# K and Q in rows of 4 or 2 tokens, reordered on the way out of PSUM; the first two FFN blocks interleaved; sink values over the SP queue

## The chip, the cores and the metric

The kernel runs on one core of a Trainium2 chip. The metric is the device time in microseconds. One execution is also taken by the hardware profiler; its span runs from the first to the last thing that the profile shows. The engines are PE (matmul; PEld is its weight load), DVE (vector), ACT (scalar), POOL and SP; each runs its own instructions in order and waits at semaphores for the others.

## The reference

Windowed attention with sinks, then a gated FFN. In short:

```python
# q, k, v: (4, 8, 768, 64); n_sink = 4, window = 128
scores = matmul(q, k^T) / sqrt(64)
keep   = (pos_k < n_sink) | ((0 <= pos_q - pos_k) & (pos_q - pos_k < window))
a      = softmax(where(keep, scores, -1e9));  attn = matmul(a, v)
x      = attn.transpose(0, 2, 1, 3).reshape(3072, 512)
g      = x @ w_gate                      # (512, 1536)
out    = (g * sigmoid(g) * (x @ w_val)) @ w_out   # (3072, 512), float32
```

Inputs are float32; the loads on POOL's queue cast them to bf16.

## The kernel before

**Attention.** The 3072 tokens are 12 groups of 256 (`NG`), three for each of 4 batches; group g has batch `b` and place `c`. For a group, `load_group` (L89, L96) loads K, Q and V with one token on each partition, so that one row read from memory is 64 floats, 256 bytes. Then come, per pair of heads p where nothing else is said:

- `step_T` (L206): four 128x128 transposes of K and Q into one PSUM tile `pt`, evicted by ACT (L213) or, for odd p before the FFN begins, by DVE (L211) into `kqT`, which holds features on partitions and the 768 tokens of a batch in order.
- `step_ks` (L221, L223), once a batch: sink columns of K into `ks`, and `vsb` = `vc` times `diag_h`, a block-diagonal copy of the sink rows of V. `vc` is loaded by 32 small loads (L185) behind all others that are issued before the FFN.
- `step_S` (L242): scores in one two-bank PSUM tile `s`, exponential on ACT (L247), mask on DVE (L251).
- `step_K` (L261, L266): scores of the sinks for a group with c > 0, and their exponential `es`.
- `step_PV` (L286), four a group: the weighted sum of V, with sums of weights from a column of ones in `va`; reciprocal and scaling on DVE (L291, L292) into `xn`.
- `step_X` (L304), two a group: transposes `xn` back to `xT` (L307), the FFN's input.

**FFN.** A block has 512 tokens, two groups. It has 12 `gate` units (four matmuls `pg` L340, tanh on ACT L343, four matmuls `pv` L348, then `u` L352 and `ht` L353 on DVE) and 4 `down` units (12 matmuls `pd` L363, eviction on ACT L367, store on SP L368). `pg`, `pv` and `pd` share three PSUM tiles, `ps_f`. Gate weights come in four chunks of three units, `wo` in four.

**Order.** All is written out by hand: `tc.manual_schedule()` leaves the engines' orders as the code issues them. Groups 0 and 1 run first, alone. Then, while block tb runs, the steps of groups 2tb+2 and 2tb+3 stand in its 16 units, by a list `slots`; within a gate they stand between pg and pv. DVE work of a step goes to `later` and is issued at the unit's end (`flush`), but evictions L211 and L213 are issued in place. The loads are issued on POOL in this order: group 0, group 1, gate weights, group 2, `wo`, group 3, `vc`; groups 4 and up when the transposes of the group four before are done. Eight loads of POOL's queue can be under way.

Of the kernel before, what the change touches and what calls it, by code (L numbers as in the profile page):

```python
# [15 lines left out]
def kernel(  # L16
# [26 lines left out]
    TB = 512  # L43
    NTB = NTOK // TB
    VS = 72
    FG = 3
# [10 lines left out]
    natp = pool("natp", 4)  # L57
    vpool = pool("vpool", 1)
    kqtp = pool("kqtp", 2)
    epool = pool("epool", 3)  # L60
# [3 lines left out]
    xtp = pool("xtp", 2)  # L64
# [6 lines left out]
    ps_o = pool("ps_o", 2, True)  # L71
    ps_t = pool("ps_t", 1, True)
# [6 lines left out]
    def load_group(g, split=1):  # L79
        b, c = divmod(g, GC)  # L80
        t0 = c * 256
        kq = natp.tile([P, 2, 2, H * D], BF16, tag="kq", name="kq")
        va = vpool.tile([P, 2, H, VS], BF16, tag=f"va{g}", name="va")
        hn = H // split
        for s in range(split):
            hs = slice(s * hn, (s + 1) * hn)
            for i, src in ((0, k), (1, q)):
                for j in range(2):
                    nc.gpsimd.dma_start(  # L89
                        kq[:, i, j, s * hn * D:(s + 1) * hn * D].rearrange(  # L90
                            "p (h d) -> p h d", d=D),
                        src[b, hs, t0 + j * P:t0 + (j + 1) * P].rearrange(
                            "h p d -> p h d"),
                    )
        for j in range(2):
            nc.gpsimd.dma_start(  # L96
                va[:, j, :, 0:D],
                v[b, :, t0 + j * P:t0 + (j + 1) * P].rearrange("h p d -> p h d"),
            )
        nat[g], vas[g] = kq, va  # L100
# [3 lines left out]
    def load_gate(i):  # L104
        n = FG * P
        for lst, w, nm in ((wgs, moe_w_gate, "wg"), (wvs, moe_w_val, "wv")):
            t = wpool.tile([P, DMC, n], BF16, tag=f"{nm}{i}", name=nm)
            nc.gpsimd.dma_start(
                t, w[:, i * n:(i + 1) * n].rearrange("(c p) f -> p c f", p=P))
            lst.append(t)  # L110
# [14 lines left out]
    vcs, vsbs, kss = [], [], []  # L125

    load_group(0, split=2)
    make_identity(nc, ident)


    def build_mask(m, sink):
# [19 lines left out]
    load_group(1)  # L151
    build_mask(mask0, True)
    load_gate(0)
    load_gate(1)
    build_mask(mask, False)
    load_gate(2)
    load_gate(3)
    load_group(2)


    nc.gpsimd.memset(diag_h, 1.0)
    nc.gpsimd.affine_select(
        out=diag_h, in_=diag_h, compare_op=ALU.is_ge, fill=0.0, base=0,
        pattern=[[-NS, H]], channel_multiplier=1)
    nc.gpsimd.affine_select(
        out=diag_h, in_=diag_h, compare_op=ALU.is_ge, fill=0.0, base=NS - 1,
        pattern=[[NS, H]], channel_multiplier=-1)
    KS = P + 2 * NS
    for b in range(B):
        vc = const.tile([P, D + 1], BF16, tag=f"vc{b}", name="vc")  # L170
        nc.vector.memset(vc, 0.0)
        nc.vector.memset(vc[:, D:D + 1], 1.0)
        ks = const.tile([P, NP2 * KS], BF16, tag=f"ks{b}", name="ks")
        nc.vector.memset(ks, 0.0)
        vsb = const.tile([P, H, D + 1], BF16, tag=f"vsb{b}", name="vsb")
        vcs.append(vc)
        kss.append(ks)
        vsbs.append(vsb)

    for i in range(4):  # L180
        load_out(i)
    load_group(3)
    for b in range(B):
        for h in range(H):
            nc.gpsimd.dma_start(vcs[b][h * NS:(h + 1) * NS, 0:D], v[b, h, 0:NS])  # L185

    def ones_v(g):
        nc.vector.memset(vas[g][:, :, :, D:D + 1], 1.0)
# [10 lines left out]
    def step_T(g, p, on_dve=False):  # L199
        b, c = divmod(g, GC)  # L200
        if c == 0 and p == 0:
            kqT[b] = kqtp.tile([P, NP2, 2, S], BF16, tag="kqT", name="kqT")
        pt = ps_t.tile([P, 2, 2, P], BF16, tag="pt", name="pt")
        for i in range(2):
            for t in range(2):
                nc.tensor.transpose(  # L206
                    pt[:, i, t], nat[g][:, i, t, p * P:(p + 1) * P], ident)
        dst = kqT[b][:, p, :, c * 256:(c + 1) * 256].rearrange(
            "q i (t r) -> q i t r", t=2)
        if on_dve:  # L210
            nc.vector.tensor_copy(out=dst, in_=pt)  # L211
        else:
            nc.scalar.copy(out=dst, in_=pt)  # L213

    def step_ks(g):

        b = g // GC
        dst = kss[b].rearrange("q (a m) -> q a m", m=KS)
        for h in range(2):
            r = slice(h * D, (h + 1) * D)  # L220
            nc.vector.tensor_copy(  # L221
                out=dst[r, :, h * NS:(h + 1) * NS], in_=kqT[b][r, :, 0, 0:NS])
        nc.vector.tensor_tensor(  # L223
            vsbs[b],
            vcs[b].rearrange("q (o d) -> q o d", o=1).broadcast_to([P, H, D + 1]),
            diag_h.rearrange("q (h o) -> q h o", o=1).broadcast_to([P, H, D + 1]),
            op=ALU.mult)
# [27 lines left out]
    def step_K(g):  # L255
# [3 lines left out]
        ps = ps_t.tile([P, 256], FP32, tag="pt", name="pk")  # L259
# [8 lines left out]
    def step_PV(g, j, hh):  # L268
# [4 lines left out]
        po = ps_o.tile([P, 4, D + 1], FP32, tag="o", name="o")  # L273
# [23 lines left out]

    def step_X(g, j):
        tb, off = divmod(g * 256 + j * P, TB)
        if off == 0:  # L300
            xTs[tb] = xtp.tile([P, DMC, TB], BF16, tag="xT", name="xT")
        pt = ps_t.tile([P, DMC, P], BF16, tag="pt", name="px")
        for i in range(DMC):
            nc.tensor.transpose(pt[:, i], xns[g, j][:, i * P:(i + 1) * P], ident)  # L304

        def dve():
            nc.vector.tensor_copy(out=xTs[tb][:, :, off:off + P], in_=pt)  # L307
        later.append(dve)

    def T(g, p):  # L310
        def f(pro=False):
            if p == 0:
                ones_v(g)
            step_T(g, p, on_dve=(pro and p % 2 == 1))
            if p == NP2 - 1:
                if g % GC == 0:
                    later.append(lambda: step_ks(g))
                if g + 4 < NG:
                    load_group(g + 4)
        return f  # L320

    def A(fn, *a):
        def f(pro=False):
            if pro and fn is not step_S:
                flush()
            fn(*a)
        return f
# [4 lines left out]
    def gate(tb, f, attn):  # L332
        fi, fo = divmod(f, FG)
        fs = slice(fo * P, (fo + 1) * P)
        if f == 0:
            hts[tb] = hpool.tile([P, DFC, TB], BF16, tag="ht", name="ht")
        x = xTs[tb]
        pg = ps_f.tile([P, TB], FP32, tag="f", name="pg")
        for c in range(DMC):
            nc.tensor.matmul(pg, wgs[fi][:, c, fs], x[:, c],  # L340
                             start=(c == 0), stop=(c == DMC - 1))
        th = tpool.tile([P, TB], FP32, tag="th", name="th")
# [3 lines left out]
        pv = ps_f.tile([P, TB], FP32, tag="f", name="pv")  # L346
        for c in range(DMC):
            nc.tensor.matmul(pv, wvs[fi][:, c, fs], x[:, c],  # L348
                             start=(c == 0), stop=(c == DMC - 1))

        u = upool.tile([P, TB], BF16, tag="u", name="u")
        nc.vector.scalar_tensor_tensor(u, th, 1.0, pg, op0=ALU.add, op1=ALU.mult)  # L352
        nc.vector.tensor_tensor(hts[tb][:, f], u, pv, op=ALU.mult)  # L353
        flush()

    def down(tb, ts, attn):
        po = ps_f.tile([P, DM], FP32, tag="f", name="pd")
        n = DFC // 4
        for f in range(DFC):
            if f == DFC // 2:  # L360
                for a in attn:
                    a()
# [5 lines left out]
        nc.sync.dma_start(out[tb * TB + ts * P:tb * TB + (ts + 1) * P], ot)  # L368
        flush()


    def run(*steps):
        for s in steps:
            s(pro=True)
# [3 lines left out]
    def ts(g):  # L378
        return [T(g, p) for p in range(NP2)], [A(step_S, g, p) for p in range(NP2)]

    def px(g):
        return ([A(step_PV, g, j, hh) for j in range(2) for hh in range(2)],
                [A(step_X, g, j) for j in range(2)])

    t0, s0 = ts(0)
    t1, s1 = ts(1)
    v0, x0 = px(0)
    v1, x1 = px(1)
    run(*t0)
    run(s0[0], s0[1], s0[2], t1[0], s0[3], t1[1], t1[2], t1[3])  # L390
    run(v0[0], s1[0], v0[1], s1[1], v0[2], s1[2], v0[3], s1[3],
        A(step_K, 1), x0[0], x0[1])
    run(*v1, *x1)
    flush()
    for tb in range(NTB):
        slots = [[] for _ in range(16)]
        if tb + 1 < NTB:
            ga, gb = 2 * tb + 2, 2 * tb + 3
            ta, sa = ts(ga)
            tb_, sb = ts(gb)  # L400
            va_, xa = px(ga)
            vb, xb = px(gb)
            slots = [
                [ta[0], ta[1]], [ta[2], ta[3]], [sa[0]], [sa[1], A(step_K, ga)],
                [sa[2], tb_[0]], [sa[3], tb_[1]], [va_[0], tb_[2]],
                [va_[1], tb_[3]], [va_[2], sb[0], A(step_K, gb)], [va_[3], sb[1]],
                [xa[0], sb[2]], [xa[1], sb[3]],
                [vb[0], vb[1]], [vb[2], vb[3], xb[0]], [xb[1]], [],
            ]
        for f in range(DFC):  # L410
            gate(tb, f, slots[f])
        for s in range(TB // P):
            down(tb, s, slots[DFC + s])
# [35 lines left out]
```

The softmax here doesn't subtract the row's maximum and nothing guards it: scores larger than these inputs give would overflow.

## Time and profile before

| | |
|---|---|
| runs (us) | 329.96, 330.28, 327.13; median 329.96 |
| profiled execution | 327.02 us, span 325.2 us |
| granted TensorE clock | 1.00 |
| busy of the span: PE, PEld, DVE, ACT, POOL | 77%, 40%, 52%, 39%, 29% |
| chain that ended last | PE 63%, DVE 13%, DMA 9%, POOL 7%, ACT 5%, issue 2% |
| DMA | 85268 packets, of which 76544 under 512 bytes; HBM read 28.34 MB, written 6.29 MB |

Shares of busy time are means over the span; the page's second part has the span in 40 slices and shows where the work lies. In a row of groups the two last numbers before the second bar are busy time in all and the mean of one instruction. In the chain a row is start, length and what ran.

### The profile page before, as it was taken

How to read it: one execution, taken by the hardware profiler on the slowest of the kernel's cores; microseconds unless marked ns; L12 is line 12 of the kernel's file. 1: busy time of each engine (PE TensorE's matmuls, PEld its weight loads, DVE VectorE, ACT ScalarE, POOL GpSimd, SP SyncE). 2: the span in 40 equal slices, each digit the busy share in tenths (PEclk: the TensorE clock that was granted, in tenths of full speed). 3: DMA queues.
4: the chain of work that ended last, by engine and by line, in shares of the span. 5: the costliest groups of instructions: out<-in, count | busy, mean ns of one | idle time of the engine just before them, and what ended most of it. 6: DMA issues, size and time to landing. Idle time of an engine off the chain costs nothing.

```text
span 325.2 us, 4622 instructions
## 1 busy us (share of the span) xinstructions
PE 251.2 (77%) x1824; PEld 128.8 (40%) x1824; DVE 167.9 (52%) x352; ACT 127.2 (39%) x197; POOL 95.8 (29%) x142
## 2 busy tenths in 40 slices
PE   0420000576999988999979999799997999999995
PEld 0210000353454544555434545345453454544442
DVE  2200000663788526886158882378842688617830
ACT  1230000324665136762257541475514666223321
POOL 8996756996532006050042600000000000000000
PEclk9999999999999999999999999999999999999999
DMA  8999999099929129390149932100011000020002
GB/s 56 113 132 203 173 203 90 1 72 124 100 15 84 40 92 73 24 99 30 69 54 78 75 24 90 39 2 3 1 65 67 0 2 0 34 94 3 2 32 97
DMA packets 85268, 20.75 MB, mean 64 GB/s; under 512 B 76544, under 2 KB 82176, under 8 KB 85248
## 3 DMA queue, kind: packets, MB, share of 16 engines
q0 software_dynamic: 81792, 14.18, 55.3%
q1 hardware_dynamic: 3456, 6.29, 5.0%
q8 instruction: 14, 0.23, 0.3%
q14 instruction: 6, 0.05, 0.0%
HBM read 28.34 MB, written 6.29 MB: 107 GB/s over the span
## 4 chain that ended last, share of the span: by engine, by line
PE 63%; DVE 13%; DMA 9%; POOL 7%; ACT 5%; issue 2%; DVEq 0%; POOLq 0%
PE pd L363 18%; PE pv L348 16%; PE pg L340 15%; DVE ht L353 4%; PE o L286 4%; PE s L242 3%; PE pt L206 3%; DMA wg<-in_moe_w_gate_dram 3%; DMA va<-in_v_dram 3%; POOL kq L89 3%; DMA wo<-in_moe_w_out_dram 3%; DVE e L251 2%; DVE u L352 2%; ACT th L343 2%; PE px L304 2%
## 5 line engine op out<-in xcount | busy, mean ns | idle before, releaser
L340 PE MATMUL pg<-xT,wg 128*128 128x512 bf16 x288 | 73.9, 379 | 0.5 <-DVE xT L307 0.5
L348 PE MATMUL pv<-xT,wv 128*128 128x512 bf16 x288 | 74.1, 380 | 0.0
L352 DVE SCALAR_TENSOR_TENSOR u<-th,pg 128x512 bf16<-128x512 f32 x72 | 49.4, 686 | 40.8 <-ACT th L343 39.9
L343 ACT ACTIVATE th<-pg 128x512 f32<-128x512 f32 x72 | 43.0, 597 | 69.4 <-PE pg L340 69.4
L206 PE MATMUL pt<-ident,kq 128*128 128x128 bf16 x192 | 20.2, 233 | 61.2 <-DVE kqT L211 39.9
L363 PE MATMUL pd<-wo,ht 128*128 128x512 bf16 x288 | 65.6, 379 | 0.0
L353 DVE TENSOR_TENSOR ht<-u,pv 128x512 bf16<-128x512 bf16 x72 | 49.5, 688 | 24.1 <-PE pv L348 19.5
L247 ACT ACTIVATE e<-s 128x1024 bf16<-128x1024 f32 (+1 forms) x48 | 45.6, 950 | 9.9 <-PE s L242 9.3
L213 ACT COPY kqT<-pt 128x512 bf16<-128x512 bf16 x44 | 25.8, 585 | 54.6 <-PE pt L206 54.6
L89 POOL DMA_DIRECT2D kq<-in_k_dram x26 | 22.6, 882 | 77.7 <-PE pt L206 76.7
L340 PEld LDWEIGHTS <-wg 128*128 128x128 bf16 x288 | 28.2, 98 | 34.4 <-issue 0.6
L206 PEld LDWEIGHTS <-kq 128*128 128x128 bf16 x192 | 13.6, 103 | 67.6 <-issue 61.2
L363 PEld LDWEIGHTS <-ht 128*128 128x128 bf16 x288 | 27.4, 98 | 30.4
L367 ACT ACTIVATE ot<-pd 128x512 f32<-128x512 f32 x24 | 14.3, 597 | 60.3 <-PE pd L363 60.3
L348 PEld LDWEIGHTS <-wv 128*128 128x128 bf16 x288 | 25.0, 98 | 23.6 <-issue 3.6
L251 DVE TENSOR_TENSOR e<-e,mask 128x1024 bf16<-128x1024 bf16 (+1 forms) x48 | 30.6, 640 | 1.8 <-ACT e L247 1.8
L223 DVE TENSOR_TENSOR vsb<-vc,diag_h 128x520 bf16<-128x520 bf16 x4 | 2.8, 701 | 40.7 <-DMA vc<-in_v_dram 40.6
L89 POOL DMA_DIRECT2D kq<-in_q_dram x26 | 22.6, 885 | 0.8 <-DMA wv<-in_moe_w_val_dram 0.8
L242 PE MATMUL s<-kqT 64*128 64x128 bf16 (+1 forms) x256 | 19.6, 255 | 3.9 <-ACT e L247 3.9
L96 POOL DMA_DIRECT2D va<-in_v_dram x24 | 21.4, 915 | 3.7 <-DMA wo<-in_moe_w_out_dram 1.7
L292 DVE TENSOR_TENSOR xn<-o,rcp 128x256 bf16<-128x256 f32 x48 | 20.4, 425 | 1.7
L286 PEld LDWEIGHTS <-e 128*128 128x128 bf16 x352 | 17.7, 103 | 6.6 <-issue 0.9
(36 smaller groups left out, 126.0 us busy)
## 6 DMA issues: line engine op xcount, KB each, us to landing
out_dram<-ot SPq DMA_DIRECT2D x24, 256.0 KB, 2.0
va<-in_v_dram POOLq DMA_DIRECT2D x24, 128.0 KB, 4.5
kq<-in_k_dram POOLq DMA_DIRECT2D x22, 128.0 KB, 4.2
kq<-in_q_dram POOLq DMA_DIRECT2D x22, 128.0 KB, 4.7
wg<-in_moe_w_gate_dram POOLq DMA_DIRECT2D x4, 384.0 KB, 7.7
wv<-in_moe_w_val_dram POOLq DMA_DIRECT2D x4, 384.0 KB, 8.9
wo<-in_moe_w_out_dram POOLq DMA_DIRECT2D x4, 384.0 KB, 9.1
vc<-in_v_dram POOLq DMA_DIRECT2D x32, 0.5 KB, 1.6
```

The source lines that it names most:

```text
L89: nc.gpsimd.dma_start(kq[:, i, j, s * hn * D:(s + 1) * hn * D].rearrange("p (h d) -> p h d", d=D), src[b, hs, t0 + j * P:t0 + (j + 1) * P] ...
L206: nc.tensor.transpose(pt[:, i, t], nat[g][:, i, t, p * P:(p + 1) * P], ident)
L242: nc.tensor.matmul(ps[:, h, col:col + n], kT[r, kk:kk + P], qT[r, qq:qq + n], start=True, stop=True)
L247: nc.scalar.activation(e, ps[:, :, lo:512], AF.Exp, scale=scale)
L251: nc.vector.tensor_tensor(e, e, m[:, :, lo:512].broadcast_to([P, 2, 512 - lo]), op=ALU.mult)
L286: nc.tensor.matmul(o, l, r, start=(i == 0), stop=(i == len(mms) - 1), skip_group_check=True)
L340: nc.tensor.matmul(pg, wgs[fi][:, c, fs], x[:, c], start=(c == 0), stop=(c == DMC - 1))
L343: nc.scalar.activation(th, pg, AF.Tanh, scale=0.5)
L348: nc.tensor.matmul(pv, wvs[fi][:, c, fs], x[:, c], start=(c == 0), stop=(c == DMC - 1))
L352: nc.vector.scalar_tensor_tensor(u, th, 1.0, pg, op0=ALU.add, op1=ALU.mult)
L353: nc.vector.tensor_tensor(hts[tb][:, f], u, pv, op=ALU.mult)
L363: nc.tensor.matmul(po, hts[tb][:, f, ts * P:(ts + 1) * P], wos[f // n][:, f % n], start=(f == 0), stop=(f == DFC - 1))
```

## The change

It has these parts:

- **Loads.** K and Q come by batch in two parts: part A, tokens 0 to 511, four tokens on each partition (rows of 1024 bytes), and part B, tokens 512 to 767, two on each (512 bytes). A load covers four heads. `natp` has two tiles of each part. V stays as it was.
- **Transposes.** A transpose of 128 columns takes two tokens of one head, so its result has even tokens on the lower 64 partitions and odd ones on the upper. A step has eight transposes. A part-A step evicts one head parity with one 64x1024 copy on ACT (even tokens) and one on DVE (odd ones); a part-B step evicts both parities, with two 64x512 copies on each. The copies write every second token of `kqT`, whose layout stays. Four A-steps and two B-steps serve a batch; the order of steps is no longer by group.
- **Sinks.** Eight small loads on SP's queue bring the sinks of all batches into `vcf` (float32), first of all; the four `vsb` products are made before the first eviction on DVE, and `diag_h` is built early on POOL.
- **Blocks.** Seven, of 512, 256, 512, 512, 512, 512 and 256 tokens. Gate weights come in chunks of 1, 2, 3, 3 and 3 units. The order of loads is: A and V of the first two groups, four gate chunks, B of batch 0, V of group 2, the last gate chunk, A of batch 1, `wo`, then the rest.
- **Order of the first blocks.** Gates 0 to 8 of block 0 with nothing between; then group 2 by itself; then gates 0 to 8 of block 1; gates 9 to 11 of both in turn; then the six downs. The T, S, PV and X steps of groups 3 and 4 stand in units 18 to 30 of these 31. Later blocks carry the steps of two groups in their units (`pair`), blocks 5 and 6 together those of group 11. A down spreads its steps over its matmuls and flushes after each.
- **PSUM.** `ps_t` and `ps_o` become one pool `ps_a` of three tiles for T, K, PV and X.

The core of the diff:

```diff
-    TB = 512
-    FG = 3
+    SIZES = [512, 256, 512, 512, 512, 512, 256]
+    PARTS = ((0, 4), (512, 2))
+    FCH = [1, 2, 3, 3, 3]
...
-    ps_o = pool("ps_o", 2, True)
-    ps_t = pool("ps_t", 1, True)
+    ps_a = pool("ps_a", 3, True)
...
+    def load_kq(b, a, k2):
+        t0, r = PARTS[a]
+        if k2 == 0:
+            nat[b, a] = natp.tile([P, 2, H, r * D], BF16, tag=f"kq{a}", name="kq")
+        hs = slice(4 * k2, 4 * k2 + 4)
+        for i, src in ((0, k), (1, q)):
+            nc.gpsimd.dma_start(
+                nat[b, a][:, i, hs],
+                src[b, hs, t0:t0 + r * P].rearrange("h (p r) d -> p h (r d)", r=r))
...
+    nc.vector.memset(vcf, 0.0)
+    nc.vector.memset(vcf[:, :, D:D + 1], 1.0)
+    for h in range(H):
+        nc.sync.dma_start(
+            vcf[h * NS:(h + 1) * NS, :, 0:D],
+            v[:, h, 0:NS].rearrange("b s d -> s b d"))
+    load_kq(0, 0, 0)
...
+    load_kq(0, 0, 1)
     build_mask(mask0, True)
+    load_v(0)
     build_mask(mask, False)
+    load_v(1)
+    for i in range(4):
+        load_gate(i)
+    load_b(0)
+    load_v(2)
+    load_gate(4)
+    load_a(1)
+    for i in range(4):
+        load_out(i)
+    load_v(3)
+    load_v(4)
+    load_b(1)
+    load_v(5)
...
-    for b in range(B):
-        for h in range(H):
-            nc.gpsimd.dma_start(vcs[b][h * NS:(h + 1) * NS, 0:D], v[b, h, 0:NS])
...
+    def step_T(b, a, n):
+        t0, r = PARTS[a]
+        pt = ps_a.tile([P, 8, P], BF16, tag="a", name="pt")
+        if r == 4:
+            k2, hs = n // 2, (n % 2,)
+        else:
+            k2, hs = n, (0, 1)
+        m = 0
+        for h in hs:
+            for p in (2 * k2, 2 * k2 + 1):
+                for i in range(2):
+                    for s_ in range(r // 2):
+                        nc.tensor.transpose(
+                            pt[:, m],
+                            nat[b, a][:, i, 2 * p + h, 2 * s_ * D:2 * (s_ + 1) * D],
+                            ident)
+                        m += 1
+        for h in hs:
+            dst = kqT[b][h * D:(h + 1) * D, 2 * k2:2 * k2 + 2, :,
+                         t0:t0 + r * P].rearrange(
+                "q a i (p s u) -> q (a i) s p u", s=r // 2, u=2)
+            for u in range(2):
+                src = pt[u * D:(u + 1) * D]
...
+                if u == 0:
+                    nc.scalar.copy(out=d, in_=src)
+                else:
+                    nc.vector.tensor_copy(out=d, in_=src)
...
+    pro(T0[0], T0[1], S0[0], S0[1], S1[0], S1[1], T0[2], T0[3], S0[2], S0[3],
+        S1[2], S1[3])
+    flush()
+    step_K(1)
+    pro(*V0)
+    flush()
+    pro(V1[0], *X0, *V1[1:])
+    flush()
+    pro(*X1)
+    flush()
...
+    us = ([(gate, 0, f) for f in range(9)] + [(alone, 0, 0)]
+          + [(gate, 1, f) for f in range(9)]
+          + [(gate, tb, f) for f in range(9, 12) for tb in (0, 1)]
+          + [u for u in units(0, 1) if u[0] is down])
+    add(sl, *((9, a) for a in (*Tb(0), *s2, A(step_K, 2), *v2, *x2)))
+    add(sl, *zip((18, 19, 20, 21), t1), (20, s3[0]), (21, s3[1]), (22, s3[2]),
+        (23, s3[3]))
...
+    add(sl, *zip((4, 5, 6, 7), ta_))
+    weave(units(2), sl)
+    sl = pair(7, 8)
+    add(sl, *zip((3, 5), Tb(2)), *zip((9, 10, 11, 12), Ta(3)))
+    weave(units(3), sl)
+    sl = pair(9, 10)
+    add(sl, *zip((11, 12), Tb(3)))
+    weave(units(4), sl)
```

## The prediction

> **What bounds the kernel now.** I read the page's slices first, then the table of waits, then the chain that ended last, then the windows. The slices say that the kernel has two lives:
>
> ```profile
> PE   0420000576999988999979999799997999999995
> ...
> DVE  2200000663788526886158882378842688617830
> ...
> DMA  8999999099929129390149932100011000020002
> GB/s 56 113 132 203 173 203 90 1 72 124 100 15 84 40 92 73 24 99 30 69 54 78 75 24 90 39 2 3 1 65 67 0 2 0 34 94 3 2 32 97
> ```
>
> A slice is 8.13 us. In slices 4 to 7 (24 to 57 us) PE and DVE do nothing and only the loads move; from slice 10 on PE is nearly full. The waits name the holder:
>
> ```profile
> ACT kqT L213 <- PE pt L206: 54.6, 13, 39.8
> DVE vsb L223 <- DMA vc<-in_v_dram: 40.6, 1, 40.6
> PE pt L206 <- DVE kqT L211: 39.9, 2, 39.4
> ```
>
> Each line: who waited, for whom, total us, times, longest. These are one wait seen three times (the longest of each). DVE stands 40.6 us at L223 (`vsb`), because the sink values `vc` are the last of POOL's queue, behind all weights and four groups. DVE runs in order, so the eviction L211 behind L223 waits too; PE needs its PSUM tile, and ACT needs PE. The chain gives the dates:
>
> ```profile
> 43.89 9.66 DMA va<-in_v_dram
> 54.42 1.59 DMA vc<-in_v_dram
> 56.14 0.70 DVE vsb L223
> ...
> 74.40 1.04 PE pg L340 x4
> ...
> 117.55 0.88 PE pg L340 x4
> ...
> 161.29 0.88 PE pg L340 x4
> ...
> 290.54 0.86 PE pg L340 x4
> ...
> 311.26 10.37 PE pd L363 x48
> ```
>
> So the first FFN matmul starts at 74.4 us, of which the wait takes up to 56. Block starts in the whole chain are 74.40, 117.55, 161.29, 203.80, 246.79 and 290.54. The last block has no attention beside it and takes 321.63 - 290.54 = 31.09 us. The other five take 43.15, 43.74, 42.51, 42.99 and 43.75, so their ten groups of attention add 60.7 us, 6.07 a group. The windows show what fills such a block:
>
> ```profile
> 117.50:161.30 43.80, 41.49 (x322) 21.41 (x320) 26.93 (x54) 22.03 (x34) 10.51 (x12) 1.00 0.63 61
> ```
>
> (columns: length, then busy time of PE, PEld, DVE, ACT, POOL, granted clock, DMA share, GB/s). PE is busy 41.5 of 43.8; DVE has 17 us spare in total. Check of the model: 74.4 + 6 x 31.09 + 60.7 + 3.6 (from the last matmul's end to the span's end) = 325.2, the span.
>
> **The change, part by part.**
>
> *Sinks.* The 32 `vc` loads (0.50 us each on POOL, 15.9 us) go. Eight SP loads into `vcf` replace them. An out store takes 0.33 us on SP's queue, so eight are issued by about 1.5 + 2.6 = 4.1 us and land, at the stores' 2.0 us, by 6.1. The four `vsb` products then stand on DVE ahead of all evictions: 4 x 0.70 = 2.8 us, done at 8.9. That ends the 40.6 us wait. What is late next is the data and the serial work of groups 0 and 1, so I walk that. (The three later `vsb` products leave the gates; two of them lie on the chain shown by the trace: -1.5 us.)
>
> *Loads.* A part-A load brings 256 KB with rows of 1024 bytes instead of 64 to 128 KB with rows of 256. The rates seen are 113 GB/s (slice 2, K and Q in short rows) and 203 (slice 4, weights, 1536-byte rows). The first two loads are issued at 1.3 and 2.1 us; the first 64 KB before landed 2.7 us after issue. 512 KB then land at 6.0 (203 GB/s) or 7.2 (113). I take 6.0, as the new rows are nearer to the weights'. POOL reaches the weights at about 14 us in the new order. Up to gate chunk 3 there are 3.9 MB, up to the last `wo` 8.1 MB; at 150 GB/s (what before averaged: 7.9 MB by 54 us) they are in at 28 and 56 us. They are needed near 50 and 83 us (below), so I cost the transfers at nothing; they cover down to 100 GB/s.
>
> *Evictions.* The transposes of a group stay 16, and PE pays nothing new. But before, 48 evictions of 128x512 took 0.585 us on ACT (44) or 0.42 on DVE (4). Now each batch has four A-steps (64x1024 on ACT and 64x1024 on DVE) and two B-steps (two 64x512 on each). No row writes with a step of two elements. The bounds come from these rows (last numbers: busy us and mean ns):
>
> ```profile
> L247 ACT ACTIVATE e<-s 128x1024 bf16<-128x1024 f32 x32 | 32.7, 1021 | 5.7 <-PE s L242 5.3
> ...
> L251 DVE TENSOR_TENSOR e<-e,mask 128x1024 bf16<-128x1024 bf16 x32 | 21.9, 685 | 1.8 <-ACT e L247 1.8
> ...
> L292 DVE TENSOR_TENSOR xn<-o,rcp 128x256 bf16<-128x256 f32 x48 | 20.4, 425 | 1.7
> ...
> L223 DVE TENSOR_TENSOR vsb<-vc,diag_h 128x520 bf16<-128x520 bf16 x4 | 2.8, 701 | 40.7 <-DMA vc<-in_v_dram 40.6
> ...
> L211 DVE COPY kqT<-pt 128x512 bf16<-128x512 bf16 x4 | 1.7, 424 | 12.6 <-PE pt L206 12.6
> ```
>
> DVE has two slopes. Dense bf16 costs 0.685 us for 1024 elements and 0.424 for 512; f32, and the broadcast bf16 of `vsb`, cost 0.425 for 256 and 0.70 for 520, that is 1.05 ns more for each element, so 1.22 us for 1024 and 0.69 for 512. I take the slow end, because `vsb` is bf16 and still slow, and like the new copy it is not dense. DVE gains 16 x 1.22 + 16 x 0.69 - 1.7 = 28.9 us (fast end: 16.1). ACT: 16 x 1.02 + 16 x 0.585 = 25.7, as before (25.8).
>
> [...]
>
> The changed kernel's instruction order shows something that the diff does not: each DVE eviction of a step waits for ACT's, and in a B-step ACT's second waits for DVE's first. So they run one after the other.
>
> *Startup walked.* Tiles at 6.0; T0 and T1 of batch 0 on PE till 7.6; ACT 7.1 to 9.1; DVE 8.9 to 11.3 (two of 1.22); four S steps at the trace's periods of 1.40 (group 0) and 1.72 (group 1) till 17.6; T2 and T3: ACT to 19.7, DVE to 21.2; four more S steps to 27.5, K inside; then V0 2.4, V1 and X0, X1 as before (K to first gate took 8.0 us there, with 1.5 us of other work): the first gate at **36** us. Ends: 33 (faster loads, dense-rate evictions) and 42 (loads at 113 GB/s, sinks at the longest `vc` landing of 6.7 us).
>
> *Group 2 alone.* At unit 9 the FFN stops and group 2 runs by itself with nothing to hide it: two B-steps until ACT is free 3.8, four S of 1.72 to 10.1, `es` 0.4, V 2.9, X 2.1 = **15.5** (13 to 18).
>
> *FFN and groups 3 to 11.* FFN 6 x 31.09 = **186.5**, wherever the interleaving puts it. Two blocks of 256 tokens: a gate there is PE 0.86, DVE 2 x 0.425, and with three PSUM tiles the round trip pg, tanh 0.38, u, ht is about 0.95, so 0.09 x 24 = **+2** (0 to 4). Nine groups at 6.07 = **54.6**. Block 2 starts right behind the last X of group 4: **+1**.
>
> *Evictions in the gates.* 16 of the 18 later T-steps stand in gates. The next pv needs pg's PSUM tile, freed by u: pg 0.86 + tanh 0.60 + ACT 1.02 + DVE 1.22 + u 0.69 + hand-overs 0.25 = 4.6 us, where PE has 3.7 us of work: 0.9 lost, 14.4 in all. Before, the paired T units took 3.27 us (117.55 to 120.82) instead of 2.33, 0.94 a group, already in the 6.07: 8.5 for nine. Net **+6** (0 with the fast slope, +12 if each unit waits once more).
>
> *Sum.* 36 + 186.5 + 15.5 + 2 + 54.6 + 1 + 6 - 1.5 + 3.6 = 303.7 us of span; with the 1.8 us around it (327.02 - 325.2), **305.5**. The profiled run lies 2.9 us under the median of 329.96; I give 305.5 and keep those 3 us for the range.
>
> **The rivals.**
>
> *Nothing is given back (0.17).* The evictions hide in DVE's spare 17 us a block, and small tiles cost nothing: 305.5 - 6 - 2 - 1 = 296.5. For it: the spare time. Against: the spare lies in the down stage, and the T-steps lie in gates.
>
> *The start stays late (0.13).* Sinks through SP share the DMA engines with POOL's 1 MB of K and Q; if they land at 18 instead of 6 us, DVE stands and the first gate moves by about 9 more: 315. Against: `vc` took 1.6 us at the median amid heavy loads.
>
> *The evictions bind: slower (0.05).* Place: the kqT evictions of the step-2 write. If half-width strided writes cost s times my rows on both engines, the path gains 2.24(s-1) in 16 gates, 3.46(s-1) twice in the startup and 3.2(s-1) in group 2: 46(s-1). It decides from s = 1.47 (46 x 0.47 = 21.5, the whole gain); s = 2 gives 351. For it: no such row exists. Against: even 64x16 copies into ks take 0.17 us.
>
> *The transfers bind: slower (0.03).* At slice 1's 56 GB/s `wo` lands at 147 instead of the needed 83: 305.5 + 64 = 370; it decides below 78 GB/s (8.1 MB by 104 us). Against: 56 is a slice in which POOL issued 64 KB every 0.75 us; the later load slices reach 90 to 203.
>
> **How the numbers follow.** My forecast has 0.60 and runs from 300 to 312. The range 293 to 319 takes in the first two rivals and leaves out the two slower ones. A measurement of this kernel tells about 1% from no change. Faster by over 1%: 0.60 + 0.17 + 0.13 = 0.90; slower: 0.05 + 0.03 = 0.08; the 0.02 left stand for a milder form of those two, within 1%.
>
> **What would show it.** Right: the wait of DVE on the sinks is gone or under 8 us; first pg at 33 to 42 us; a PE hole of some 15 us behind nine gates; 64x1024 copies at 1.22 us on DVE and 1.02 on ACT; gates with a T-step near 3.3 us; granted clock 1.00 as now. Wrong: a first pg after 45 us (which load or engine ended the wait is the cause), a wait of PE on wg, wv or wo, a DVE copy over 1.8 us, or a block of two groups over 47 us.

## The result and the profile after

The changed kernel takes 340.38 us at the median of four runs (338.74 to 342.46); the kernel before 329.15, also of four. The ratio is 1.035, with a 95% interval of 1.026 to 1.044: slower. The forecast was 305.5 us and faster. The profiled execution took 342.46 us with a span of 340.7, the forecast's sum was 303.7: 37 us are to be found.

The slices of the changed kernel (8.5 us each):

```profile
PE   1142899369557997755699978658999999999995
...
DVE  2837747657678444768882667687389774888600
ACT  1674123623682524585332735645356435533221
...
PEclk9999999769897999999799979989999999999999
DMA  8999999990049112900002000000300011000022
```

The hole of slices 4 to 7 is gone. In its place PE has dents at slices 8 and 9 (group 2 alone), 11 and 12 (the part-A steps of batch 1), 16 to 20 (block 2) and 24 to 28 (block 3). The granted clock, which the profile shows as 1.00 all through before, dips in or just behind these dents (lowest in slice 9, a 6). The waits of the changed kernel (who, for whom, total us, times, longest):

```profile
DVE kqT L257 <- ACT kqT L255: 31.4, 22, 3.5
...
PE pv L392 <- DVE u L396: 21.6, 10, 3.7
...
PE s L280 <- DVE kqT L257: 16.6, 7, 4.1
...
DVE vsb L206 <- DMA vcf<-in_v_dram: 5.0, 1, 5.0
```

The sink wait is 5.0 us instead of 40.6. What replaced it are the evictions into `kqT`: DVE's copy (L257) waits for ACT's (L255), PE's scores wait for DVE's copy, and `pv` waits for `u`, which stands behind that copy. The groups by shape show why (last numbers: busy us, mean ns):

```profile
L257 DVE COPY kqT<-pt 64x1024 bf16<-64x1024 bf16 x16 | 38.9, 2430 | 18.2 <-ACT kqT L255 18.0
L255 ACT COPY kqT<-pt 64x1024 bf16<-64x1024 bf16 x16 | 38.9, 2428 | 18.5 <-PE pt L237 18.4
...
L257 DVE COPY kqT<-pt 64x512 bf16<-64x512 bf16 x16 | 11.7, 732 | 13.5 <-ACT kqT L255 13.4
L255 ACT COPY kqT<-pt 64x512 bf16<-64x512 bf16 x16 | 11.5, 722 | 11.4 <-DVE kqT L257 8.6 <-PE pt L237 2.8
```

A part-A copy of 1024 takes 2.43 us on either engine, where I had 1.02 for ACT and 1.22 for DVE; a part-B copy of 512 takes 0.72 to 0.73 (0.585 and 0.69). One such step in a gate of block 2, in the timeline (start, length, engine, line):

```profile
144.17 0.61 PE L237 MATMUL pt<-ident,kq 128*128 128x128 bf16 x8
...
145.21 2.43 ACT L255 COPY kqT<-pt 64x1024 bf16<-64x1024 bf16 x1
...
147.68 2.43 DVE L257 COPY kqT<-pt 64x1024 bf16<-64x1024 bf16 x1 [3.54 <-ACT kqT L255]
...
150.12 0.69 DVE L396 SCALAR_TENSOR_TENSOR u<-th,pg 128x512 bf16<-128x512 f32 x1
150.86 1.02 PE L392 MATMUL pv<-xT,wv 128*128 128x512 bf16 x3 [3.47 <-DVE u L396]
```

Transposes, ACT's copy, DVE's copy, `u`, `pv`: ACT's copy starts when ACT has done its exponentials, and from there each starts as the one before ends. This `pv` is the next gate's; it needs the PSUM tile of `pg` that `u` sets free, and PE stood 3.47 us ahead of it.

### The profile page after: what moved, and what is told of

Same layout as the page of the kernel before. It is cut to its first block, busy times and chain, and to the rows that moved or that the text cites. A ratio compares the mean times of both kernels' runs of the same rounds, so it can differ in the third digit from the quotient of the medians.

```text
span 340.7 us, 4805 instructions
## 1 busy us (share of the span) xinstructions
PE 265.3 (78%) x1891; PEld 142.3 (42%) x1920; DVE 220.1 (65%) x398; ACT 155.0 (45%) x197; POOL 61.1 (18%) x92
## 3 DMA queue, kind: packets, MB, share of 16 engines
q0 software_dynamic: 48736, 14.16, 39.5%
## 4 chain that ended last, share of the span: by engine, by line
PE 57%; DVE 21%; ACT 16%; issue 2%; DMA 2%; POOL 0%; DVEq 0%; ACTq 0%; POOLq 0%
PE pd L410 16%; PE pg L384 15%; PE pv L392 15%; DVE kqT L257 14%; ACT kqT L255 9%; PE s L280 4%; ACT e L285 4%; DVE u L396 4%; PE o L324 3%; ACT th L387 2%; PE pt L237 2%; PE px L348 2%; DMA kq<-in_q_dram 2%; DVE ht L397 1%; DVE xn L330 1%
## 5 line engine op out<-in xcount | busy, mean ns | idle before, releaser
L392 PE MATMUL pv<-xT,wv 128*128 128x512 bf16 (+1 forms) x321 | 79.4, 362 | 23.6 <-DVE u L396 21.6
L387 ACT ACTIVATE th<-pg 128x512 f32<-128x512 f32 (+1 forms) x84 | 45.3, 539 | 90.9 <-PE pg L384 80.4
L384 PE MATMUL pg<-xT,wg 128*128 128x512 bf16 (+1 forms) x331 | 79.4, 361 | 1.8 <-DVE xT L351 1.0
L257 DVE COPY kqT<-pt 64x1024 bf16<-64x1024 bf16 (+1 forms) x32 | 50.6, 1581 | 31.7 <-ACT kqT L255 31.4
L396 DVE SCALAR_TENSOR_TENSOR u<-th,pg 128x512 bf16<-128x512 f32 (+1 forms) x84 | 51.2, 610 | 25.4 <-ACT th L387 24.0
L255 ACT COPY kqT<-pt 64x1024 bf16<-64x1024 bf16 (+1 forms) x32 | 50.4, 1575 | 30.0 <-PE pt L237 21.2
L397 DVE TENSOR_TENSOR ht<-u,pv 128x512 bf16<-128x512 bf16 (+1 forms) x84 | 51.4, 612 | 11.3 <-PE pv L392 2.6
L392 PEld LDWEIGHTS <-wv 128*128 128x128 bf16 x336 | 31.0, 99 | 47.9 <-issue 31.4
L237 PE MATMUL pt<-ident,kq 128*128 128x128 bf16 x192 | 16.8, 242 | 16.3 <-DVE kqT L257 8.4
L280 PEld LDWEIGHTS <-kqT 64*128 64x128 bf16 x256 | 9.4, 100 | 43.9 <-issue 27.7
L93 POOL DMA_DIRECT2D kq<-in_k_dram x16 | 12.3, 771 | 63.4 <-PE pt L237 59.0
```

Source lines behind the costliest of these rows:

```text
L237: nc.tensor.transpose(pt[:, m], nat[b, a][:, i, 2 * p + h, 2 * s_ * D:2 * (s_ + 1) * D], ident)
L255: nc.scalar.copy(out=d, in_=src)
L257: nc.vector.tensor_copy(out=d, in_=src)
L280: nc.tensor.matmul(ps[:, h, col:col + n], kT[r, kk:kk + P], qT[r, qq:qq + n], start=True, stop=True)
L384: nc.tensor.matmul(pg, wgs[fi][:, c, fs], x[:, c, 0:n], start=(c == 0), stop=(c == DMC - 1))
L387: nc.scalar.activation(th, pg, AF.Tanh, scale=0.5)
```

## The experiments

My theory after the first profile: the price of the part-A copies makes the whole difference, and the price comes from how far apart their writes lie. The rivals: half-width reads by two engines, the chain of waits itself, the loads, or the interleaving. In each expectation theory A is the one that I held and theory B its rival; they have nothing to do with the parts A and B of the loads.

**e1_step2: the same copies, walked in another order.** A four-token partition puts token 4p + 2s + u at place 2s + u. For one u, the copy ran over p inside s: each write lay four elements (8 bytes) behind the last. Run over s inside p, the writes are two elements apart.

```diff
-                "q a i (p s u) -> q (a i) s p u", s=r // 2, u=2)
+                "q a i (p s u) -> q (a i) p s u", s=r // 2, u=2)
...
-                    src = src.rearrange("q (x s) p -> q x s p", s=2)
+                    src = src.rearrange("q (x s) p -> q x p s", s=2)
...
-                    d = dst[:, :, 0, :, u]
+                    d = dst[:, :, :, 0, u]
```

> The changed kernel with one thing altered: the part-A evictions walk the same elements in another order, so that the innermost write step is two elements (4 bytes) instead of four (8 bytes), and the read from PSUM jumps instead. Theory A (the price of a strided copy is set by the byte step of its write; 2.43 us is the price of 8 bytes, and 1.2 that of 4): the 64x1024 copies take 1.2 to 1.3 us on both engines, blocks 2 and 3 fall from 57 to 45 to 48 us, first gate near 37 us, time 305 to 312. Theory B (half-width reads of PSUM by two engines, or any strided copy of 1024, cost 2.4 us whatever the write step; or the chain of waits, not the copies, is what costs): copies stay at 2.4 us and the time at 340; if copies fall but the time stays over 330, the waits are the cause.

Measured: 312.36 us (310.9 to 312.88), ratio to before 0.953 [0.949, 0.956]. By shape:

```profile
L257 DVE COPY kqT<-pt 64x1024 bf16<-64x1024 bf16 x16 | 20.9, 1304 | 8.8 <-ACT kqT L255 8.5
L255 ACT COPY kqT<-pt 64x1024 bf16<-64x1024 bf16 x16 | 20.7, 1293 | 13.1 <-PE pt L237 12.9
```

Three changed lines (the third only follows the renamed axes) turn 3.5% slower into 4.7% faster: 28 us. Nothing else differs, so the order of elements makes this difference; theory B falls.

**m1_steps: the copies by themselves.** Each kind runs four times on ACT, then four times on DVE, with nothing beside them but the stores of the output in the first 21 us. The main kinds, with their lines and what they are:

```diff
+            cp(out=d[0:H, 0:1024], in_=pt[0:H])                    # L63 dense
...
+            cp(out=strided(d, 1024, 2), in_=pt[0:H])               # L65; L67 and L69: step 4 and 8
...
+            cp(out=strided(d, 1024, 4, P), in_=pt)                 # L71: 128 partitions, step 4
...
+            cp(out=strided(d, 512, 2), in_=pt[0:H, 0:512])         # L76; L78: step 4
...
+            cp(out=d[0:H, 0:512], in_=strided(pt, 512, 2))         # L80: only the read is strided
...
+            cp(out=strided(d, 1024, 4), in_=sb[0:H])               # L84: from SBUF, step 4
...
+            cp(out=strided(f, 1024, 2), in_=pt[0:H])               # L88: float32, step 2; L86 dense
```

L73, not shown here, has the views of e1_step2: a write at step 2 whose read jumps.

> Only the disputed copies, by themselves: the kernel computes nothing of the reference; it runs copies of 64 partitions from PSUM (bf16) on ACT and then on DVE, four of each kind, with write steps of 1, 2, 4 and 8 elements, 64 and 128 partitions, read steps of 2 and 4, an SBUF source, and float32 writes. Theory A (byte step of the write): 1024 elements take about 0.7 to 1.0 us at step 1, 1.2 at step 2, 2.43 at step 4 on both engines, no matter how many partitions or which source; step 8 is 2.4 if the cost saturates, 4.6 if it grows with the step. Theory B (contention of two engines in the kernel): alone, step 4 costs 1.2 us like step 2.

Measured, groups by shape:

```profile
L69 ACT COPY da<-pt 64x1024 bf16<-64x1024 bf16 x4 | 18.7, 4674 | 0.1
L69 DVE COPY dv<-pt 64x1024 bf16<-64x1024 bf16 x4 | 18.7, 4672 | 0.1
L84 ACT COPY da<-sb 64x1024 bf16<-64x1024 bf16 x4 | 9.8, 2456 | 0.1
L71 DVE COPY dv<-pt 128x1024 bf16<-128x1024 bf16 x4 | 9.7, 2420 | 0.1
...
L67 ACT COPY da<-pt 64x1024 bf16<-64x1024 bf16 x4 | 9.7, 2413 | 0.1
L67 DVE COPY dv<-pt 64x1024 bf16<-64x1024 bf16 x4 | 9.6, 2411 | 0.1
L84 DVE COPY dv<-sb 64x1024 bf16<-64x1024 bf16 x4 | 5.2, 1293 | 0.1
L65 ACT COPY da<-pt 64x1024 bf16<-64x1024 bf16 x4 | 5.1, 1284 | 0.1
L73 ACT COPY da<-pt 64x1024 bf16<-64x1024 bf16 x4 | 5.1, 1284 | 0.1
...
L65 DVE COPY dv<-pt 64x1024 bf16<-64x1024 bf16 x4 | 5.1, 1282 | 0.1
...
L86 DVE CAST fv<-pt 64x1024 f32<-64x1024 bf16 x4 | 4.9, 1222 | 0.1
L88 DVE CAST fv<-pt 64x1024 f32<-64x1024 bf16 x4 | 4.9, 1217 | 0.1
L88 ACT CAST fa<-pt 64x1024 f32<-64x1024 bf16 x4 | 4.2, 1048 | 0.1
L86 ACT CAST fa<-pt 64x1024 f32<-64x1024 bf16 x4 | 4.1, 1029 | 0.1
L63 ACT COPY da<-pt 64x1024 bf16<-64x1024 bf16 x4 | 4.0, 1005 | 0.5 <-PE pt L47 0.4
...
L63 DVE COPY dv<-pt 64x1024 bf16<-64x1024 bf16 x4 | 2.7, 682 | 83.5 <-ACT fa L88 83.4
```

From PSUM, 1024 bf16 elements take 1.0 us (ACT) or 0.68 (DVE) dense, 1.28 at step 2, 2.41 at step 4 and 4.67 at step 8, strided alike on both engines, and at step 4 with 64 or 128 partitions (2.41 and 2.42). Up to step 8 it does not saturate. The views of e1_step2 (L73) cost what a plain step 2 costs (1.284 us on ACT for both), so the jumping read adds nothing here. So neither contention nor half width is needed. Two things miss my theory: from SBUF, the memory of all tiles outside the PSUM pools, DVE pays 1.29 at step 4 and not 2.4 (ACT pays 2.46), and float32 at step 2, which is also 8 bytes apart, costs about what dense float32 does (1.05 and 1.03 on ACT, 1.22 on DVE for both). "Byte step" is thus too simple: here it holds for bf16 from PSUM.

**e3_short_rows: one token per partition again, dense copies.** Steps, blocks and order stay.

```diff
+            for j in range(r):
                 nc.gpsimd.dma_start(
-                nat[b, a][:, i, hs],
-                src[b, hs, t0:t0 + r * P].rearrange("h (p r) d -> p h (r d)", r=r))
+                    nat[b, a][:, i, hs, j * D:(j + 1) * D],
+                    src[b, hs, t0 + j * P:t0 + (j + 1) * P].rearrange("h p d -> p h d"))
...
-                "q a i (p s u) -> q (a i) s p u", s=r // 2, u=2)
+                "q a i (p s u) -> q (a i) s u p", s=r // 2, u=2)
```

> The changed kernel with K and Q loaded one token per partition again (rows of 256 bytes, 80 loads of 64 KB instead of 32), so that the same half-width evictions write dense runs of 128. Steps, blocks and their order stay. Theory A (write step): 64x1024 copies take about 1.02 us on ACT and 0.7 to 1.2 on DVE, blocks 2 and 3 about 44 us, time 300 to 308. Theory B (half width or waits): copies stay at 2.4 us or blocks at 57, time 338 to 342. Rival on the loads: short rows are late, the first gate comes after 45 us and group 2 after 65.

Measured: 298.56 us (298.27 to 298.76), 0.911 [0.909, 0.913]. First gate at 36.3 us; copies by shape:

```profile
L256 ACT COPY kqT<-pt 64x1024 bf16<-64x1024 bf16 x16 | 16.1, 1005 | 13.6 <-PE pt L238 13.3
...
L258 DVE COPY kqT<-pt 64x1024 bf16<-64x1024 bf16 x16 | 11.1, 694 | 7.1 <-ACT kqT L256 6.8
```

Giving up the long rows, and with them the strided writes, gains 42 us. PE waits 1.1 us in all for a load, and the first gate is no later than in e1_step2 (36.8).

**e5_rows: e1_step2 with rows of 256 bytes.** The same tokens come to the same places; only the loads are cut.

```diff
+            for j in range(r):
                 nc.gpsimd.dma_start(
-                nat[b, a][:, i, hs],
-                src[b, hs, t0:t0 + r * P].rearrange("h (p r) d -> p h (r d)", r=r))
+                    nat[b, a][:, i, hs, j * D:(j + 1) * D],
+                    src[b, hs, t0:t0 + r * P].rearrange("h (p r) d -> r p h d", r=r)[j])
```

> e1_step2 (312.4 us) with the same tokens in the same places, but K and Q loaded in rows of 256 bytes: one load for each of the 4 or 2 tokens of a partition. Evictions and order stay. Theory A (long rows are worth nothing here, since the first gate came at 36.8 with long and 36.3 us with short rows): 310 to 315 us, first gate 36 to 38. Theory B (long rows pay, and the dense copies of e3_short_rows hid it): first gate after 40 us or a later wait on loads, time 317 or more.

Measured: 313.39 us (312.6 to 314.44), 0.951 [0.946, 0.956], beside 312.36 for e1_step2. The first gate comes at 38.4 us instead of 36.8. The long rows are worth 1.6 us at the start and about 1 us in all, which is within the spread of the runs: with the copies equal, the loads are hidden.

**e2_sinks: the kernel before with the sink part alone.**

```diff
...
+    for h in range(H):
+        nc.sync.dma_start(
+            vcf[h * NS:(h + 1) * NS, :, 0:D],
+            v[:, h, 0:NS].rearrange("b s d -> s b d"))
     load_group(0, split=2)
     make_identity(nc, ident)
... (diag_h, then ks and the four vsb products, are moved up to here)
-            nc.gpsimd.dma_start(vcs[b][h * NS:(h + 1) * NS, 0:D], v[b, h, 0:NS])
```

> The kernel before with the sink part of the change alone: sinks over SP into vcf, vsb made ahead of the evictions, diag_h early. Theory A (the sink wait of 40.6 us is a plain gain, and the changed kernel lost it by its other parts): first gate near 36 us instead of 74.4, the six blocks as before, time 327 - 38 = 289, up to 295 if a block waits for a load. Theory B (the loads that lay behind the wait come out as a new wait on wg, wv, wo or group 2's tiles, so the weight-by-weight interleaving was needed): first gates hold on DMA, time 305 to 320.

Measured: 293.98 us (293.83 to 295.78), 0.899 [0.895, 0.903]. The sink part alone is worth 34 us; the first gate comes at 36.8 us instead of 74.4. Block 0 takes 47.9 us instead of 43.2. In its first gate PE waits for group 2's K and Q, 1.9 us in three waits, and the matmuls before and behind them run at about half speed (four in 1.86 and 1.91 us, 1.03 elsewhere):

```profile
36.79 1.86 PE L340 MATMUL pg<-xT,wg 128*128 128x512 bf16 x4 [0.52 <-DVE xT L307]
...
39.68 0.29 PE L211 MATMUL pt<-ident,kq 128*128 128x128 bf16 x1 [0.69 <-DMA kq<-in_k_dram]
40.64 0.29 PE L211 MATMUL pt<-ident,kq 128*128 128x128 bf16 x1 [0.67 <-DMA kq<-in_q_dram]
41.51 0.29 PE L211 MATMUL pt<-ident,kq 128*128 128x128 bf16 x1 [0.57 <-DMA kq<-in_q_dram]
...
42.84 1.91 PE L348 MATMUL pv<-xT,wv 128*128 128x512 bf16 x4
```

The mean granted clock that the profile shows for this execution is 0.999, so what slowed these matmuls is not shown. So theory A, and a little of B: the loads behind the old wait do show, but for less than 5 us.

**e6_sinks_g2 and e7_sinks_g23: the order of loads.** e6 puts group 2 ahead of gate chunks 2 and 3, e7 also group 3 ahead of `wo`.

```diff
+    load_group(2)
     load_gate(2)
     load_gate(3)
-    load_group(2)
...
+    load_group(3)      # e7 only
     for i in range(4):
         load_out(i)
-    load_group(3)
```

> e2_sinks (294.0 us) with group 2's loads issued ahead of gate chunks 2 and 3. There block 0 took 47.9 us, and its first gate stood some 5 us on K and Q of group 2 (landed at 39 to 41 us). Theory A (that is the only new wait): block 0 takes 43.2 us as in the kernel before, time 289 to 290. Theory B (the gate chunks, now later, hold units 6 to 11): time 293 to 295 with a wait on wg or wv.

> e6_sinks_g2 (293.6 us) with group 3's loads ahead of the four wo loads as well. In e6 the wait only moved: PE stood at 51 to 55 us on K and Q of group 3, behind wo in the queue, and then ran at half speed for some 4 us; block 0 took 50.2 us in its profile. wo is first needed near 70 us. Theory A (each block waits for the load that stands last before its use, and with this order none does): block 0 takes 43 to 44 us, time 288 to 290. Theory B (the 8 MB take what they take, and the wait moves on to gate chunks or wo): 292 to 294.

Measured: e6 293.59 us, no better than e2; the wait had moved to the next group (timeline of e6, PE; the profiled execution was its slowest, 296.08 us):

```profile
51.69 0.23 PE L211 MATMUL pt<-ident,kq 128*128 128x128 bf16 x1 [1.41 <-DMA kq<-in_k_dram]
53.09 0.29 PE L211 MATMUL pt<-ident,kq 128*128 128x128 bf16 x1 [1.16 <-DMA kq<-in_k_dram]
```

No chunk of weights was waited for, so both theories of e6 miss the place. e7: 288.29 us, 0.877 [0.872, 0.883], block 0 at 42.6 us: behind the first tile no PE wait on a load is left in this order, as its theory A said.

**e8_psum: e7 with one PSUM pool of three tiles**, as in the change.

```diff
-    ps_o = pool("ps_o", 2, True)
-    ps_t = pool("ps_t", 1, True)
+    ps_a = pool("ps_a", 3, True)
```

> e7_sinks_g23 with one more part of the change: ps_t and ps_o become one pool of three tiles. In the kernel before, a gate with two T-steps takes 3.27 us where its PE work is 2.33, because the second T waits for ACT's eviction of the first from the one tile of ps_t. Theory A (that wait is PE time lost): two such gates in each of five blocks give back up to 0.9 us each and the startup some 2 us, time 5 to 10 us under e7. Theory B (the wait covers ACT and DVE work that then holds pv instead): within 2 us of e7.

Measured: 276.64 us (275.96 to 277.48), 0.839 [0.835, 0.844]; 11.7 us under e7, a little over what theory A gave. The two gates with paired T-steps take 2.2 us each instead of 3.3. Two middle blocks in the windows (length, PE, PEld, DVE, ACT, POOL busy, granted clock):

```profile
79.09:120.15 41.06, 41.06 (x322) 21.48 (x321) 26.80 (x54) 21.80 (x34) 10.50 (x12) 1.00 0.68 65
120.15:159.97 39.82, 39.76 (x298) 20.23 (x297) 26.79 (x56) 20.44 (x33) 10.50 (x12) 1.00 0.69 67
```

PE is busy over nearly all of both; blocks 1 to 4 are 2.7 us shorter than in e7 each, and that is the gain. The first gate comes 4.4 us earlier, at 32.2 us, but block 0 loses 4.3 of it: it takes 46.9 us, with four waits on group 3's K and Q (2.8 us) and a granted clock of 0.93.

This is the fastest version: the kernel before with the sinks over SP, the better order of loads and the one pool. e3_short_rows, the changed kernel with dense copies, also has the sinks and the pool and takes 22 us more. What of this lies with the evictions in the gates, the first two blocks interleaved or the small blocks was not taken apart.

**e4_woven: e1_step2 with group 2 inside the gates** of block 0 instead of by itself.

```diff
-    us = ([(gate, 0, f) for f in range(9)] + [(alone, 0, 0)]
-    add(sl, *((9, a) for a in (*Tb(0), *s2, A(step_K, 2), *v2, *x2)))
+    add(sl, *zip((0, 0), Tb(0)), *zip((1, 2, 3, 4), s2), (4, A(step_K, 2)),
+        *zip((5, 5, 6, 6), v2), *zip((7, 7), x2))
```

> e1_step2 (312.4 us) with group 2's steps set into gates 0 to 7 of block 0, between pg and pv, instead of by themselves after gate 8. Theory A (group 2 alone is a hole of some 15 us which also drops the granted clock to 0.7 there): the stretch goes, its PE work of about 6 us comes into the gates, mean granted clock near 1.00, time 301 to 305. Theory B (the gates then pay it back by evictions and DVE work, or group 2's K and Q are not there at 37 us): gain under 4 us, time 308 to 312, or a wait of PE on kq in the first gate.

Measured: 308.1 us (307.1 to 308.44), 0.935 [0.931, 0.939]: 4.3 us under e1_step2, where I had 7 to 11. From the first gate to block 2 it takes 74.6 us instead of 78.8. K and Q were there; the two B-steps in the first gate held the next gate's `pv` (timeline of e4):

```profile
44.61 1.40 PE L392 MATMUL pv<-xT,wv 128*128 128x512 bf16 x4 [2.77 <-DVE u L396]
45.80 1.91 PE L384 MATMUL pg<-xT,wg 128*128 128x512 bf16 x4
```

The matmuls behind that wait ran at half speed (four in 1.91 us; 1.03 elsewhere), at a granted clock of 0.51 (a window of e4 with the columns of e8):

```profile
45.20:48.60 3.40, 3.40 (x15) 1.01 (x13) 2.25 (x5) 0.84 (x2) 1.25 (x2) 0.51 1.25 208
```

The hole is mostly paid back, as theory B said.

**e9_later: e1_step2 with DVE's half of the evictions behind u and ht** for batches 1 to 3.

```diff
-                    nc.vector.tensor_copy(out=d, in_=src)
+                    if b == 0:
+                        nc.vector.tensor_copy(out=d, in_=src)
+                    else:
+                        later.append(lambda d=d, src=src: nc.vector.tensor_copy(out=d, in_=src))
```

> e1_step2 (312.4 us) with DVE's half of each eviction of batches 1 to 3 issued at the end of its unit, behind u and ht, instead of in front of them. Theory A (the loss in a gate with a T-step is u standing behind the DVE copy, which itself stands behind ACT's): the 12 A-steps and 4 of the 6 B-steps that lie in gates or downs lose about 0.7 to 1.0 us less each, time 299 to 304, blocks 2 and 3 at 43 to 46 instead of 48 and 51 us. Theory B (DVE is simply full in these gates: the copy delays the next unit's u instead): time 308 to 312.

Measured: 302.79 us (301.76 to 303.66), 0.918 [0.913, 0.923], 9.6 us under e1_step2. Blocks 2 and 3 in the windows:

```profile
117.50:161.50 44.00, 41.04 (x314) 21.15 (x313) 34.72 (x63) 24.20 (x33) 4.74 (x6) 1.00 0.29 43
161.50:206.50 45.00, 42.49 (x337) 22.37 (x336) 35.21 (x62) 25.62 (x34) 0.00 (x0) 1.00 0.07 25
```

They take 44 and 45 us instead of 48.2 and 51.1 with the same DVE work (34.7 and 35.2 us busy, 34.6 and 35.1 in e1). So the loss in a gate is `u` standing behind the copies, not a full DVE.

## Why the prediction was wrong

The sum, spread over the stages, beside the two kernels' spans (us, rounded; block starts from the timeline of PE):

| stage | forecast | changed | e1_step2 |
|---|---|---|---|
| first gate | 36.0 | 42.9 | 36.8 |
| gates 0 to 8 of block 0 | 15.5 | 17.3 | 15.7 |
| group 2 alone | 15.5 | 16.0 | 16.3 |
| rest of blocks 0 and 1 | 47.0 | 54.0 | 46.8 |
| block 2 | 46.8 | 56.5 | 48.2 |
| block 3 | 45.9 | 57.9 | 51.1 |
| block 4 (no A-step) | 42.3 | 39.4 | 39.4 |
| blocks 5 and 6 | 52.8 | 53.1 | 53.1 |
| after the last matmul, `vsb` | 3.6 - 1.5 | 3.6 | 3.6 |
| span | 303.7 | 340.7 | 311.1 |

**The step that failed is the price of the part-A evictions.** I wrote "No row writes with a step of two elements" and priced all new copies by rows with other steps, 1.22 us on DVE. Two things were wrong in it. First, only the part-B copies write at step 2 in their innermost loop. In part A the loop over p is innermost and a partition holds four tokens, so the step is 4; the diff's `rearrange` says so, and I did not read it. Second, I took 1.22 us as an upper bound because the rows of before showed no third slope, and gave ACT no price for a stride at all. The copies cost 2.43 us on both. The dense rows bounded the cost of this access pattern from below only. Of the 37 us, the step of four makes 30 (340.7 - 311.1 between the spans); the other 7 are smaller errors of the sum. With the order of elements turned, the same kernel lands at 312.4 us, within the given range, and stage by stage near the sum but for block 3. Two of the signs that I had named for being wrong were there: a DVE copy over 1.8 us, and blocks of two groups over 47 us.

**The rival was the right one, with too small a chance.** "The evictions bind" decided from s = 1.47; the part-A copies had 2.43 / 1.02 = 2.4 on ACT and 2.43 / 1.22 = 2.0 on DVE. With both together, s = 4.86 / 2.24 = 2.17, its formula would give 46 x 1.17 = 54 us; the span came out 37 over the sum. The formula counts 16 gates, but only 11 of them hold part-A steps; the part-B copies had only 1.2 and 1.06. And the place that the rival named, a write at step 2, would not have decided: the part-A copies of e1_step2 have s = (1.29 + 1.30) / 2.24 = 1.16.

**What held.** The sinks: the wait is 5.0 us, the `vsb` products end at 10.6 us (8.9 forecast), and alone they are worth 34 us (e2). The startup walk: 36.8 us in e1 for 36, though its start was off: the first tile of K and Q was complete at 7.6 us, behind even the slow case of 7.2, and later steps won half of that back. Group 2 alone: 16.0 for 15.5. Loads at no cost: no wait of PE on wg, wv or wo, and row length is worth about 1 us (e5). The one-after-the-other of ACT and DVE, and `u` behind them (e9). Block 4 came 2.9 us under the forecast, and e8 explains a part of it: there the one pool of three PSUM tiles took 2.7 us from a block, where my sum had taken off 1.9 for the paired T-steps (0.94 a group). The rest stays open.

**What I sized wrong besides.** Blocks 2 and 3 stay 1.4 and 5.2 us over the forecast in e1, so 0.9 us for each T-step in a gate is too low with copies of 1.30. And the granted clock was not 1.00: in the changed kernel

```profile
59.50:77.00 17.50, 9.39 (x100) 6.41 (x99) 10.55 (x22) 8.07 (x11) 7.48 (x10) 0.71 1.40 128
...
130.30:187.00 56.70, 42.91 (x310) 21.93 (x313) 39.15 (x63) 28.57 (x34) 4.74 (x6) 0.97 0.22 33
187.00:244.70 57.70, 45.66 (x331) 23.46 (x336) 39.60 (x62) 29.79 (x34) 0.00 (x0) 0.94 0.05 19
244.70:284.20 39.50, 38.82 (x277) 18.97 (x280) 28.81 (x56) 19.28 (x29) 0.00 (x0) 1.00 0.08 28
```

group 2 alone, with PE busy 9.39 of 17.5 us, got 0.71, and the stalled blocks 2 and 3 got 0.97 and 0.94; block 4, with PE busy 38.82 of 39.5 us, got 1.00. The profile does not show it lower behind every hole in PE's work: the first 42.9 us of this kernel, with PE busy 16.38, also have 1.00. So what lowers the clock is not shown. How many of the 37 us the clock took was not measured by itself. Estimated from the mean that the profile shows, it was at most (1 - 0.959) x 340.7 = 14 us of PE time, and (1 - 0.977) x 311.1 = 7 in e1_step2; so some 7 of the 30 us between these two can be the clock's.

**On DVE's slow end.** The slow slope that I took gave 1.22 us, and a copy at step 2 is near it: 1.28 us, where a dense one takes 0.68 (m1_steps). But the cost does not stop there: step 4 (2.41 us) takes nearly twice as long as step 2, and step 8 (4.67) nearly four times. The distance in bytes alone does not set it: float32 at step 2, 8 bytes apart, costs about what dense float32 does (1.05 and 1.03 us on ACT), while bf16 pays at 4 bytes already (1.28 us for 1.00 on ACT).

**What stays open.** Why 2-byte writes from PSUM pay nearly in proportion to their step from step 2 to step 8 (1.28, 2.41 and 4.67 us) and 4-byte writes at step 2 do not (1.05 us for 1.03 on ACT), and why DVE pays half as much from SBUF (1.29 us for 2.41 at step 4). Whether the changed kernel would gain if both halves of an eviction ran at once was not tried: every second element of the same tile is written by each engine, and the schedule puts them in a row.

## What to carry to other kernels

Before pricing a rearranged copy, write down the innermost loop of its write and that loop's step; a view that reads like "every second token" can step by four. If the same elements can be walked in an order with a smaller step, take it: here that was 28 us for three lines. And a long wait found by the profile should be taken away by itself first: the sink loads alone made the kernel 10% faster, and the other parts in sum gave it all back.

## What the runs showed of the hardware that I had not expected

- Copies of 1024 bf16 elements from PSUM: 1.28, 2.41 and 4.67 us at write steps of 2, 4 and 8 elements, equal on ACT and DVE, at step 4 equal for 64 and 128 partitions (2.41 and 2.42 us). 512 elements at step 2 took 0.72 us, at step 4 1.28.
- A read at step 2 from PSUM cost ACT nothing (0.578 us for 512 bf16 elements, 0.585 dense in the kernel before); DVE took 0.682 us for it, and 0.424 dense.
- K and Q rows of 256 bytes and of 1024 and 512 bytes give the same time within about 1 us (313.4 and 312.4) in this kernel, where other work hides the loads.
